# Six scatter views, adjacent x rows, later early weights and a new load order in a fused attention and expert kernel

## The chip, the cores and the metric

One core of one Trainium2 chip runs the kernel. The metric is device time in microseconds (us) of one execution; lower is better. The kernel before took 263.31, 264.16 and 266.78 us in three runs, median 264.16 us.

## The reference

Attention in chunks of 64 tokens feeds a mixture of eight experts with a capacity of 80 tokens each. All data is fp32: q, k and v are (8, 8, 576, 64), so x has 4608 rows (tokens) of 512.

```python
scores = scale * np.matmul(q_c, k_c.transpose(0, 1, 2, 4, 3))
scores = scores - np.max(scores, axis=-1, keepdims=True)
attn = np.exp(scores)
attn = attn / (np.sum(attn, axis=-1, keepdims=True) + 1e-09)
out = np.matmul(attn, v_c)
...
x = np.ascontiguousarray(attn_out.transpose(0, 2, 1, 3)).reshape(B * S, H * D)
...
logits = x @ w_gate
expert_idx = np.argmax(logits, axis=1)
...
gate_w = probs[np.arange(N), expert_idx]
out = np.zeros((N, D), dtype=np.float32)
for e in range(E):
    ...
    if len(tok_idx) > capacity:
        gw = gate_w[tok_idx]
        keep = np.argpartition(-gw, capacity)[:capacity]
        tok_idx = tok_idx[keep]
    h = np.maximum(x[tok_idx] @ w1[e], 0.0)
    out[tok_idx] = gate_w[tok_idx, None] * (h @ w2[e])
```

So at most 640 of the 4608 output rows are not zero.

## The kernel before

The program has three stages, written in a fixed order by hand (`manual_schedule`): each engine runs its own list, and SP's list is also the list of nearly all DMAs.

**Attention (lines 550 to 711).** 18 steps `j`, each of 256 tokens. A step loads q and k (`load_qk`, line 274: `qk` of 512 KB with c=0, and with c=1 `qz`, 256 KB twice, into one of two zero-padded tiles `kz`) and v (`load_v`, line 283: four loads of 130 KB into `vz`). PE makes scores (lines 297 and 303), DVE takes maxima and subtracts (310, 316), PE transposes (327, tile `pt`), ACT takes the exponential (335), PE multiplies with v into the PSUM tile `o` (345), DVE divides (361), and SP writes x to DRAM scratch `xs` (365, 512 KB). Step `i` of the loop at line 615 mixes scores of pair `i` with values of pair `i-2` and the transposes of pair `i-3` for the gate. Loads for pair `i+2` are issued in step `i`: first `qk`, then v of pair `i`, then `qz`. Each pair's buffers are two deep, so a load waits for PE to have read the pair two before. SP's list has eight DMAs per step, and each DMA of SP waits besides for the landing of the one eight before it. The gate's logits give each token an expert (`mine`) and a weight; GpSimd (POOL) writes per token a row of numbers `comp` (lines 449 to 459), five columns per expert: two parts of the row number, three parts of the gate weight.

**Choice (lines 704 to 856).** A threshold per expert, ranks, and matmuls that gather the chosen tokens' `comp` rows. From these come the row numbers `gi` and, for the first two of six row groups, the gather. Eight halves of the first two experts' weights (`early_weights`, 1 MB each) are issued at lines 671 (six) and 709 (two, both of w2 of expert 1).

**Experts (lines 859 to 900).** Six row groups `r` of 128 slots (96 per expert, so group 0 holds experts 0, 0, 0, 1, group 1 holds 1, 1, 2, 2, and so on). POOL gathers rows of `xs` (line 160), PE transposes, multiplies with w1 (`layer1`, line 185, two halves), transposes, multiplies with w2 (`layer2`, line 218), DVE scales with the gate (223) into one of four tiles `ys`, and POOL scatters the rows into `out` (line 227). Iteration `r` runs layer1 of group `r` and layer2 of group `r-1`. `ahead` (line 876) issues the remaining weights, 2 MB each, and the nine 1 MB zero writes to `out` (`clear`, line 535). The first of these weight loads is held behind the gather by a copy of one column of the gathered tile into the weight tile (line 873). All six scatters come after the zero writes in the program.

A branch behind the experts (line 903) handles inputs that overflow the fast path; here it is not taken.

## Time and profile before

| | |
|---|---|
| median of 3 runs | 264.16 us |
| profiled execution, its own time | 263.37 us |
| its span on the core | 261.5 us |
| PE busy | 221.5 us (85%) |
| DVE busy | 124.6 us (48%) |
| ACT busy | 72.1 us (28%) |
| POOL busy | 34.9 us (13%) |
| DMA moved | 85.02 MB, mean 325 GB/s |

The span is the time between the first and the last instruction of the program in the profile; the execution's own time is 1.87 us longer. Busy shares are means over three stages with different limits, so they are read by stage. "DMA share" is the mean busy share of the 16 DMA engines; PEclk is the granted TensorE clock as a share of full speed, 1.00 or 0.50. In a wait, `<-` names what ended it.

### The profile page before, as it was taken

Reading aid. Unit: us, or ns where it says so; the run is one execution under the profiler, and the core shown is the slowest. Engines: PE = TensorE matmul, PEld = TensorE weight load, DVE = VectorE, ACT = ScalarE, POOL = GpSimd, SP = SyncE. Lnnn points to the kernel's source line nnn. Section 1 sums busy time; section 2 is a strip of 40 time slices with the busy share of each in tenths; the row PEclk is TensorE's granted clock in tenths of the full one; section 3 lists DMA queues with packets and bytes.
Section 4 is the critical chain, followed back from the end, with each engine's and each line's share of the span. In section 5 each row is a group of like instructions: output and inputs, shape, how many; then the busy total and the mean of one; then the engine's idle time right before and its main releaser. Section 6 shows DMA issues by size and latency. Waiting matters only on the chain. (4 is left out here: it accounts for less than half of the span.)

```text
span 261.5 us, 7696 instructions
## 1 busy us (share of the span) xinstructions
PE 221.5 (85%) x3297; PEld 137.2 (52%) x3297; DVE 124.6 (48%) x343; ACT 72.1 (28%) x123; POOL 34.9 (13%) x101
## 2 busy tenths in 40 slices
PE   6379979989998999998996899999999999995000
PEld 5368858777786878787784244242332433321000
DVE  7438859786978688786779321021121112100100
ACT  1023335463737273856520012020010201000000
POOL 4110000101011011222423041000000000001331
PEclk9989999999999999999799799999999999999655
DMA  7997999999999999989998799999999999971110
GB/s 258 290 328 215 324 344 326 344 351 355 354 356 354 369 292 315 345 283 370 418 401 313 263 402 408 405 413 417 417 419 414 410 413 412 399 298 40 66 71 31
DMA packets 31496, 85.02 MB, mean 325 GB/s; under 512 B 3744, under 2 KB 3872, under 8 KB 31456
## 3 DMA queue, kind: packets, MB, share of 16 engines
q1 hardware_dynamic: 30192, 80.99, 84.1%
q0 software_dynamic: 960, 2.88, 3.1%
q8 instruction: 28, 0.46, 0.7%
q10 hardware_dynamic: 304, 0.59, 0.6%
q14 instruction: 12, 0.10, 0.1%
HBM read 64.27 MB, written 20.45 MB: 324 GB/s over the span
## 5 line engine op out<-in xcount | busy, mean ns | idle before, releaser
L185 PE MATMUL hc<-w,xtc 128*32 128x512 f32 x384 | 44.9, 611 | 0.2 <-ACT xtc L175 0.2
L218 PE MATMUL yc<-w,htc 128*32 128x512 f32 x384 | 42.3, 592 | 0.0
L345 PE MATMUL o<-vz,pT 128*64 128x130 f32 x576 | 35.9, 276 | 0.3 <-ACT pT L335 0.3
L310 DVE TENSOR_REDUCE mx<-s 128x8 f32<-128x512 f32 x36 | 23.2, 686 | 22.2 <-PE s L303 22.0
L345 PEld LDWEIGHTS o<-vz,pT 128*64 128x64 f32 x576 | 31.6, 135 | 1.5 <-ACT pT L335 0.5
L218 PEld LDWEIGHTS yc<-w,htc 128*32 128x32 f32 x384 | 12.4, 110 | 28.3 <-issue 28.3
L335 ACT ACTIVATE pT<-pt 128x1024 f32<-128x1024 f32 x18 | 18.4, 1023 | 31.2 <-PE pt L327 31.2
L185 PEld LDWEIGHTS hc<-w,xtc 128*32 128x32 f32 x384 | 12.8, 112 | 26.4 <-issue 25.9
L303 PE MATMUL s<-kz 128*64 128x128 f32 x288 | 20.9, 286 | 6.5 <-DMA kz<-in_qz 6.2
L374 ACT COPY xT<-px 128x1024 f32<-128x1024 f32 x18 | 18.2, 1012 | 25.5 <-PE px L327 25.5
L361 DVE TENSOR_TENSOR x<-o,rc 128x768 f32<-128x768 f32 (+1 forms) x36 | 23.2, 685 | 0.4
L223 DVE TENSOR_SCALAR ysc<-yc,gatec 128x512 f32<-128x512 f32 x6 | 4.5, 751 | 39.3 <-PE yc L218 24.7
L316 DVE TENSOR_TENSOR sm<-s,mx 128x512 f32<-128x512 f32 x36 | 22.9, 679 | 0.0
L190 ACT ACTIVATE hsc<-hc 128x512 f32<-128x512 f32 x6 | 3.6, 601 | 64.9 <-PE hc L185 64.9
L303 PEld LDWEIGHTS s<-kz 128*64 128x64 f32 x288 | 16.6, 141 | 8.4 <-issue 6.5
L227 POOL DMA_INDIRECT out<-ysc,si x6 | 6.0, 993 | 90.0 <-SPq L903 75.3
L297 PE MATMUL s<-qk 64*64 64x64 f32 x576 | 12.9, 229 | 3.8 <-issue 2.6
L297 PEld LDWEIGHTS s<-qk 64*64 64x64 f32 x576 | 10.5, 139 | 10.1 <-issue 7.6
L207 DVE COPY htc<-hpc 128x512 f32<-128x512 f32 x6 | 4.2, 692 | 21.3 <-PE hpc L203 21.3
L465 ACT ACTIVATE lv<-lev_t,own 128x256 bf16<-128x256 f32 x32 | 13.8, 498 | 0.9 <-DVE own L443 0.8
L192 DVE TENSOR_SCALAR hsc<-hc 128x512 f32<-128x512 f32 x6 | 4.2, 692 | 19.8 <-PE hc L185 19.8
L327 PE MATMUL px<-ct,x 64*128 64x64 f32 x288 | 12.9, 230 | 0.2 <-ACT pT L335 0.2
(157 smaller groups left out, 224.4 us busy)
## 6 DMA issues: line engine op xcount, KB each, us to landing
w<-in_w SPq DMA_DIRECT2D x12, 2048.0 KB, 21.2
vz<-in_vv SPq DMA_DIRECT2D x72, 130.0 KB, 4.9
qk<-in_qk SPq DMA_DIRECT2D x18, 512.0 KB, 5.6
xs<-x SPq DMA_DIRECT2D x18, 512.0 KB, 5.3
out<-zero SPq DMA_DIRECT2D x9, 1024.0 KB, 16.1
kz<-in_qz SPq DMA_DIRECT2D x34, 256.0 KB, 4.9
w<-in_w SPq DMA_DIRECT2D x8, 1024.0 KB, 14.2
kz<-in_qz ACTq DMA_DIRECT2D x2, 256.0 KB, 5.8
```

The costliest lines, as they stand in the source:

```text
L185: nc.tensor.matmul(h[o:o + 32, :], lhsT=xT[r][:, b, o:o + 32], rhs=getw(groups[r][g])[0][:, b, 512 * f:512 * f + 512], start=(b == 0), sto ...
L218: nc.tensor.matmul(y[o:o + 32, :], lhsT=hT[r][c // 4][:, c % 4, o:o + 32], rhs=getw(groups[r][g])[1][:, c, :], start=(c == 0), stop=(c == ...
L297: nc.tensor.matmul(s0[64 * u:64 * u + 64, h, pr], lhsT=q[64 * h:64 * h + 64, pr, u, :], rhs=k[64 * h:64 * h + 64, pr, u, :], start=True, s ...
L303: nc.tensor.matmul(s1[64 * u:64 * u + 64, :, pr], lhsT=z[:, pr, u, 1], rhs=z[:, pr, u, 0:3:2], start=True, stop=True)
L310: nc.vector.tensor_reduce(mx[:, :, 4 * c:4 * c + 4], PR[j]['s'][c], axis=AX.X, op=ALU.max)
L316: nc.vector.tensor_tensor(sm[:, 4 * c:4 * c + 4].rearrange("p a k h -> p h a k"), PR[j]['s'][c], PR[j]['mx'][:, :, 4 * c:4 * c + 4, None]. ...
L327: nc.tensor.transpose(pm[:, u, 64 * a:64 * a + 64], src(a)[rows], ident[rows, rows])
L335: nc.scalar.activation(pT, pm, AF.Exp, scale=0.125)
L345: nc.tensor.matmul(po[64 * u:64 * u + 64, a // 3, o:o + 130].rearrange("p (h x) -> p h x", h=2), lhsT=PR[j]['pT'][:, u, 64 * a:64 * a + 64 ...
L361: nc.vector.tensor_tensor(xf[:, lo:hi].rearrange("p (b m e) -> p b m e", b=b1 - b0, m=m), po[:, b0:b1, 0:m, 0:64], rc[:, b0:b1, 0:m, None] ...
L374: nc.scalar.copy(XT[T][:, j % 2].rearrange("p a u t -> p u a t"), pm.rearrange("p u (a t) -> p u a t", a=8))
L465: nc.scalar.activation(lv, lev_t[:, C_LEV:C_LEV + 2 * P], AF.Sign, bias=own[:, rt:rt + 1], scale=-1.0)
```

## The change

1. Each of the six scatters writes through its own view of `out`; the views are declared disjoint, so the program no longer makes one scatter wait for the one before.
2. `x` is written so that the two rows of one partition lie side by side in `xs` (4 KB in one piece in place of two pieces of 2 KB). The gather's row numbers change with it, so `comp` gets a sixth column per expert: `C_V`, the place within 256 rows.
3. The last two early weight halves (both of w2 of expert 1) are issued behind the first gather. The copy that holds back the weights now writes their tile.
4. Loads of the first pairs: all of pair 0 and 1 and v of pair 0 go out on SP in order of need, the constants move to step 2 (their use, `late_constants`, from step 2 to step 4), v of pair 1 is loaded in step 1, and in every step `qz` is issued right behind `qk` and ahead of v. Some memsets move from DVE to POOL. The scores of pair 1 go to tile `o` in place of `s`.

```diff
-    comp = cp.tile([P, RT, 5, NE], BF16, name="comp")
+    comp = cp.tile([P, RT, 6, NE], BF16, name="comp")
...
+        rows = dram_disjoint_views(out, NR) if extra else None
...
             nc.gpsimd.indirect_dma_start(
-                out=out, out_offset=bass.IndirectOffsetOnAxis(ap=si[:, r:r + 1], axis=0),
+                out=rows[r] if extra else out,
+                out_offset=bass.IndirectOffsetOnAxis(ap=si[:, r:r + 1], axis=0),
...
-            ps = ps1.tile([P, 2, 512], F32, name=f"s{j}", tag="s")
+            ps = S['o'][:, 0:2] if j == 1 else ps1.tile([P, 2, 512], F32, name=f"s{j}", tag="s")
...
-                xs[256 * j:256 * j + 256].rearrange("(c p) d -> p c d", c=2), x)
+                xs[256 * j:256 * j + 256].rearrange("(p c) d -> p (c d)", c=2), xf)
...
-                for j, c0 in ((0, C_A), (1, C_B)):
+                for j, c0 in enumerate((C_B, C_A, C_V)):
...
-        def early_weights(n):
+        def early_weights(n, after=None):
...
+            if after is not None:
+                nc.gpsimd.tensor_copy(w[:, 2 * j, 0:1], after)
...
-                    (nc.vector, nc.gpsimd)[b].memset(kz[b][:, o:o + 512], 0.0)
-            load_qk(0, 1, nc.scalar)
+                    (nc.vector if b == 0 and o == 0 else nc.gpsimd).memset(
+                        kz[b][:, o:o + 512], 0.0)
+            load_qk(0, 1)
             nc.scalar.dma_start(ident, cst[:, C_ID:C_ID + P])
...
+            for c in range(2):
+                load_qk(1, c)
...
-                    nc.vector.memset(vz[b, c], 0.0)
+                    (nc.gpsimd if b else nc.vector).memset(vz[b, c], 0.0)
+            for c in range(2):
+                load_v(0, c)
...
-                if i == 2:
+                if i == 4:
                     late_constants()
                 scores(i)
-                load_qk(i + 2, 0)
+                for c in range(2):
+                    load_qk(i + 2, c)
                 maxima(i)
...
-                if i >= 2:
+                if i >= 1:
                     for c in range(2):
                         load_v(i, c)
-                load_qk(i + 2, 1)
+                if i == 2:
+                    constants()
...
             divide(17)
-            for n in (6, 7):
-                early_weights(n)
             threshold(ph, misc[:, 1, 0:NE])
...
             def ahead(r, xg):
 
+                if r == 0:
+                    for n in (6, 7):
+                        early_weights(n, xg[0][:, 0:1] if n == 6 else None)
...
-                        part(e, l, xg[0][:, 0:1] if r + n == 0 else None)
+                        part(e, l)
```

**Where the instructions stand.** POOL at the end of the program, before. `xgc` is a gathered tile, `w` a weight tile, `ysc` a scaled result, DMASW and DMAHW are landings of POOL's and of SP's and ACT's DMAs.

```order
L160 DMA xgc_2791<-xs,gic_2656 128x512 [waits DMAHW2_49,DMAHW1_49,DMAHW5_49,DMAHW0_49,DVE_49]
L873 COPY w_2_2799<-xgc_2791 128x1 [waits DMAHW6_49,DMAHW7_49,DMAHW3_49,DMASW0_49]
...
L227 DMA out<-ysc_3014,si 4608x512 [waits DMAHW4_49,DMAHW3_49,DMAHW5_49,DMAHW1_49,DMAHW7_49,DMAHW0_49,DVE_49]
L227 DMA out<-ysc_3111,si 4608x512 [waits DMASW6_49,DVE_49]
L227 DMA out<-ysc_3214,si 4608x512 [waits DMASW7_49,DVE_49]
L227 DMA out<-ysc_3322,si 4608x512 [waits DMASW0_49,DVE_49]
L227 DMA out<-ysc_3425,si 4608x512 [waits DMASW1_49,DVE_49]
L227 DMA out<-ysc_3463,si 4608x512 [waits DMASW3_49,DMASW2_49,DVE_49]
```

The same place on POOL now.

```order
L163 DMA xgc_2797<-xs,gic_2662 128x512 [waits DMAHW2_49,DMAHW1_49,DMAHW5_49,DMAHW0_49,DVE_49]
L552 COPY w_1_2204<-xgc_2797 128x1 [waits DMASW0_49]
...
L230 DMA out<-ysc_3022,si 4608x512 [waits DMAHW4_49,DMAHW3_49,DMAHW5_49,DMAHW1_49,DMAHW7_49,DMAHW0_49,DVE_49]
L230 DMA out<-ysc_3119,si 4608x512 [waits DVE_49]
L230 DMA out<-ysc_3222,si 4608x512 [waits DVE_49]
L230 DMA out<-ysc_3330,si 4608x512 [waits DVE_49]
L230 DMA out<-ysc_3433,si 4608x512 [waits DVE_49]
L230 DMA out<-ysc_3471,si 4608x512 [waits DMASW3_49,DVE_49]
```

Scatters 1 to 4 lost their wait for a landing of POOL's DMAs; the last one keeps one. The first still waits for the zero writes.

SP's DMAs at the start, before (`kz` takes `qz`, `vz` takes v; ACT issued the two `qz` loads of pair 0):

```order
L278 DMA qk_103<-in_qk 128x1024
L278 DMA qk_166<-in_qk 128x1024
L281 DMA kz_108<-in_qz 64x1024 [waits Pool_49] x2
L286 DMA vz_119<-in_vv 64x520 [waits DVE_49]
...
L591 DMA ct<-in_cst 128x524 [waits DMAHW3_49]
L592 DMA lev_t<-in_cst 128x642 [waits DMAHW4_49]
...
L286 DMA vz_123<-in_vv 64x520 [waits DMAHW7_49,DVE_49]
...
L278 DMA qk_209<-in_qk 128x1024 [waits DMAHW3_49,PE_49]
```

SP's DMAs at the start now:

```order
L282 DMA qk_103<-in_qk 128x1024
L285 DMA kz_106<-in_qz 64x1024 [waits DVE_49]
L285 DMA kz_106<-in_qz 64x1024 [waits Pool_49]
L282 DMA qk_115<-in_qk 128x1024
L285 DMA kz_109<-in_qz 64x1024 [waits Pool_49] x2
L290 DMA vz_120<-in_vv 64x520 [waits DVE_49]
...
L282 DMA qk_201<-in_qk 128x1024 [waits DMAHW3_49,PE_49]
L285 DMA kz_106<-in_qz 64x1024 [waits DMAHW4_49,PE_49]
```

Pair 0 is complete ahead of pair 1, and pair 2 stands directly behind v of pair 0, with constants and v of pair 1 later.

SP around the gather, before (`w_0`, `w_1`, `w_2` are weights of experts 0, 1, 2):

```order
L547 DMA w_0_2194<-in_w 128x2x1024 [waits DMAHW7_49]
L547 DMA w_0_2194<-in_w 128x2x1024 [waits DMAHW0_49]
L365 DMA xs<-x_2290 128x2x512 [waits DMAHW1_49,DVE_49]
L365 DMA xs<-x_2402 128x2x512 [waits DMAHW2_49,DVE_49]
L547 DMA w_1_2198<-in_w 128x2x1024 [waits DMAHW3_49]
L547 DMA w_1_2198<-in_w 128x2x1024 [waits DMAHW4_49]
L874 DMA w_2_2799<-in_w 128x4x1024 [waits DMAHW5_49,PE_49,Pool_49]
```

SP around the gather now:

```order
L553 DMA w_0_2200<-in_w 128x2x1024 [waits DMAHW7_49]
L553 DMA w_0_2200<-in_w 128x2x1024 [waits DMAHW0_49]
L369 DMA xs<-x_2296 128x1024 [waits DMAHW1_49,DVE_49]
L369 DMA xs<-x_2409 128x1024 [waits DMAHW2_49,DVE_49]
L553 DMA w_1_2204<-in_w 128x2x1024 [waits DMAHW3_49,Pool_49]
L553 DMA w_1_2204<-in_w 128x2x1024 [waits DMAHW4_49]
L880 DMA w_2_2808<-in_w 128x4x1024 [waits DMAHW5_49,PE_49]
```

The wait for POOL's copy, and so for the gather, moved from the first weight of expert 2 to the last two halves of expert 1.

## Rows read from the trace of the kernel before

**Rows 1.** Timeline of POOL, gathers and scatters: start, duration, what, idle before.

```profile
139.76 1.27 POOL L160 DMA_INDIRECT xgc<-xs,gic  x1 [7.12 <-DVE bt L808]
144.30 0.19 POOL L873 COPY w<-xgc 128x1 f32<-128x1 f32 x1 [1.97 <-DMA xgc<-xs,gic]
...
153.21 1.00 POOL L160 DMA_INDIRECT xgc<-xs,gic  x1 [0.31 <-issue]
...
236.33 1.02 POOL L227 DMA_INDIRECT out<-ysc,si  x1 [75.33 <-SPq L903]
241.95 1.00 POOL L227 DMA_INDIRECT out<-ysc,si  x1 [4.60 <-DMA out<-ysc,si]
245.45 0.99 POOL L227 DMA_INDIRECT out<-ysc,si  x1 [2.50 <-DMA out<-ysc,si]
...
256.00 0.98 POOL L227 DMA_INDIRECT out<-ysc,si  x1 [2.49 <-issue]
```

**Rows 2.** Timeline of DVE, the scaling by the gate of groups 4 and 5.

```profile
241.26 0.75 DVE L223 TENSOR_SCALAR ysc<-yc,gatec 128x512 f32<-128x512 f32 x1 [11.82 <-PEq L903]
244.78 0.75 DVE L223 TENSOR_SCALAR ysc<-yc,gatec 128x512 f32<-128x512 f32 x1 [2.77 <-DMA out<-ysc,si]
```

**Rows 3.** Timeline of PE, expert stage.

```profile
144.38 0.63 PE L173 MATMUL xpc<-ct,xgc 128*128 128x128 f32 x4 [3.04 <-DMA xgc<-xs,gic]
...
145.26 5.16 PE L185 MATMUL hc<-w,xtc 128*32 128x512 f32 x32 [0.24 <-ACT xtc L175]
...
151.16 7.11 PE L185 MATMUL hc<-w,xtc 128*32 128x512 f32 x64
...
215.97 3.62 PE L185 MATMUL hc<-w,xtc 128*32 128x512 f32 x32
...
228.57 10.51 PE L218 MATMUL yc<-w,htc 128*32 128x512 f32 x96
```

**Rows 4.** Busy us by stretch: PE, PEld, DVE, ACT, POOL, then PEclk, DMA share, GB/s.

```profile
0.00:5.00 5.00, 2.88 (x14) 2.08 (x15) 3.54 (x7) 1.28 (x1) 2.87 (x15) 1.00 0.63 210
5.00:10.00 5.00, 3.14 (x61) 2.45 (x59) 2.02 (x4) 0.51 (x2) 0.00 (x0) 1.00 0.98 350
10.00:15.00 5.00, 2.89 (x48) 2.54 (x48) 2.01 (x4) 0.00 (x0) 2.44 (x7) 0.68 0.90 243
15.00:20.00 5.00, 3.52 (x76) 2.95 (x76) 2.48 (x4) 1.51 (x3) 0.00 (x0) 0.97 0.98 370
20.00:27.00 7.00, 6.79 (x148) 6.03 (x145) 6.61 (x12) 2.04 (x2) 0.00 (x0) 1.00 0.73 222
27.00:34.00 7.00, 6.72 (x150) 5.22 (x152) 5.87 (x12) 3.07 (x4) 0.00 (x0) 1.00 0.97 312
48.00:55.00 7.00, 6.34 (x137) 5.56 (x136) 5.41 (x15) 2.27 (x3) 0.90 (x5) 1.00 0.99 342
62.00:69.00 7.00, 6.90 (x152) 6.05 (x150) 6.44 (x18) 2.89 (x4) 0.44 (x2) 1.00 1.01 355
145.00:150.00 5.00, 4.76 (x33) 1.15 (x32) 1.26 (x7) 0.48 (x2) 0.00 (x0) 0.66 0.89 292
150.00:155.00 5.00, 5.00 (x76) 2.30 (x76) 0.77 (x6) 1.13 (x2) 2.52 (x3) 1.00 1.02 401
170.00:180.00 10.00, 10.00 (x96) 3.77 (x92) 2.14 (x3) 1.74 (x3) 0.00 (x0) 1.00 1.03 415
235.00:236.00 1.00, 1.00 (x16) 0.37 (x12) 0.00 (x0) 0.00 (x0) 0.00 (x0) 1.00 0.00 0
```

**Rows 5.** Waits from 20 to 118 us: us in total, times, longest.

```profile
PE s L303 <- DMA kz<-in_qz: 4.3, 6, 1.6
```

**Rows 6.** DMA summary of 229 to 233 us, where only zero writes move.

```profile
DMA packets 794, 1.60 MB, mean 399 GB/s; under 512 B 28, under 2 KB 28, under 8 KB 791
```

**Rows 7.** The `xs` tile: its writes (ns, first and last start), and DMA issue to landing.

```profile
L365 SPq DMA_DIRECT2D xs<-x x18: 383/537/2032, 25.5 to 123.3; - x18
...
DMA to landing us min/median/max: 3.6/5.4/16.7
```

More of the change, by code (lines that the diff above doesn't have):

```diff
@@ L6 @@
 from concourse._compat import with_exitstack
+from concourse.ap import dram_disjoint_views
 F32 = mybir.dt.float32
@@ L37 @@
 C_B = C_A + RT
-C_W8 = C_B + RT
+C_V = C_B + RT
+C_W8 = C_V + RT
 C_OOB = C_W8 + NE
@@ L114, in compact @@
     def compact(pool, pp, ptok, tag):
-        cand = pp.tile([P, 5, NE], F32, name=f"cand{tag}", tag="cand")
+        cand = pp.tile([P, 6, NE], F32, name=f"cand{tag}", tag="cand")
         for rt in range(RT):
@@ L123, in compact @@
                 start=(rt == 0), stop=(rt == RT - 1))
-        cb = pool.tile([P, 5, NE], BF16, name=f"cb{tag}", tag="cb")
+        cb = pool.tile([P, 6, NE], BF16, name=f"cb{tag}", tag="cb")
         nc.scalar.copy(cb, cand)
@@ L146, in targets @@
         gate, row, sv = (t[:, r0:r1] for t in tiles)
-        nc.vector.tensor_reduce(gate, pl[:, :, 2:5], axis=AX.X, op=ALU.add)
+        nc.vector.tensor_reduce(gate, pl[:, :, 3:6], axis=AX.X, op=ALU.add)
         nc.vector.tensor_reduce(row, pl[:, :, 0:2], axis=AX.X, op=ALU.add)
@@ L454, in parts @@
                         ct[:, c0 + rt:c0 + rt + n, None].to_broadcast(bc), op=ALU.mult)
[L455 to L458 removed]
+                p.tensor_copy(co[:, :, 3, :], kk)
+                p.tensor_tensor(r, kk, co[:, :, 3, :], op=ALU.subtract)
                 p.tensor_copy(co[:, :, 4, :], r)
+                p.tensor_tensor(r, r, co[:, :, 4, :], op=ALU.subtract)
+                p.tensor_copy(co[:, :, 5, :], r)
             return top, chosen, weight, key
@@ L551, in attention_moe @@
             load_qk(0, 0)
-            kz = {}
+            kz, vz = {}, {}
+            warm = gk.tile([P, 2 * P], BF16, name="warm", tag="lv", bufs=LV)
             for b in range(2):
@@ L555, in attention_moe @@
                 for o in (0, 1024):
-                    (nc.vector, nc.gpsimd)[b].memset(kz[b][:, o:o + 512], 0.0)
-            load_qk(0, 1, nc.scalar)
+                    (nc.vector if b == 0 and o == 0 else nc.gpsimd).memset(
+                        kz[b][:, o:o + 512], 0.0)
+            load_qk(0, 1)
             nc.scalar.dma_start(ident, cst[:, C_ID:C_ID + P])
-            io_h = gk.tile([P, P, HOT], BF16, name="io_h", tag="io_h", bufs=1)
-            lev_t = gk.tile([P, NLEV], F32, name="lev_t", tag="lev_t", bufs=1)
-            warm = gk.tile([P, 2 * P], BF16, name="warm", tag="lv", bufs=LV)
+            for c in range(2):
+                load_qk(1, c)
             nc.vector.memset(warm, 0.0)
-            nc.vector.memset(wgp[:, :, 8:32], 0.0)
-            vz = {}
             for b in range(2):
@@ L567, in attention_moe @@
                     vz[b, c] = wk.tile([P, 2, 520], F32, name=f"vz{b}{c}", tag=f"vz{b}{c}", bufs=1)
-                    nc.vector.memset(vz[b, c], 0.0)
+                    (nc.gpsimd if b else nc.vector).memset(vz[b, c], 0.0)
+            for c in range(2):
+                load_v(0, c)
+            io_h = gk.tile([P, P, HOT], BF16, name="io_h", tag="io_h", bufs=1)
+            lev_t = gk.tile([P, NLEV], F32, name="lev_t", tag="lev_t", bufs=1)
+            nc.vector.memset(wgp[:, :, 8:32], 0.0)
             pw = ps2.tile([P, 256], F32, name="pw", tag="g")
@@ L586, in attention_moe, with constants @@
                 nc.gpsimd.memset(rsts[r0][:, :, 0:1], 0.0)
-            for c in range(2):
-                load_qk(1, c)
-            for c in range(2):
-                load_v(0, c)
-            nc.sync.dma_start(ct[:, C_ID + P:], cst[:, C_ID + P:NCONST])
-            nc.sync.dma_start(lev_t, cst[:, NCONST:])
-            nc.sync.dma_start(wgp[:, :, 0:8], wg.rearrange("(b p) e -> p b e", p=P))
-            nc.sync.dma_start(capi, cap[0:1, :].broadcast_to([P, 2]))
-            for c in range(2):
-                load_v(1, c)
+            def constants():
+                nc.sync.dma_start(ct[:, C_ID + P:], cst[:, C_ID + P:NCONST])
+                nc.sync.dma_start(lev_t, cst[:, NCONST:])
+                nc.sync.dma_start(wgp[:, :, 0:8], wg.rearrange("(b p) e -> p b e", p=P))
+                nc.sync.dma_start(capi, cap[0:1, :].broadcast_to([P, 2]))
             nc.scalar.copy(id_b, ident)
@@ L747, in listed @@
                 nc.vector.tensor_reduce(
-                    kc, cand[:, 2:5, :].rearrange("p c e -> p e c"), axis=AX.X, op=ALU.add)
-                cb = mp.tile([P, 5, NE], BF16, name=f"cb{nm}", tag=f"cb{nm}")
+                    kc, cand[:, 3:6, :].rearrange("p c e -> p e c"), axis=AX.X, op=ALU.add)
+                cb = mp.tile([P, 6, NE], BF16, name=f"cb{nm}", tag=f"cb{nm}")
                 nc.scalar.copy(cb, cand)
@@ L793, in spread @@
                                         lists[n][0][:, e:e + 1].to_broadcast([P, P]), ident)
-            cands.append(ps2.tile([P, 5, NE], F32, name="candb", tag="g"))
+            cands.append(ps2.tile([P, 6, NE], F32, name="candb", tag="g"))
             gather_up(cands[1], [*range(LATE, RT)], 0, 4)
@@ L891, in remaining @@
             def remaining(pp):
-                pl, gi = place(mp, pp.tile([P, NR - 2, 5], F32, name="pl2", tag="y", bufs=1),
+                pl, gi = place(mp, pp.tile([P, NR - 2, 6], F32, name="pl2", tag="y", bufs=1),
                                pairs, "c", 2, NR)
@@ L970, in attention_moe @@
                         cand, cb = compact(xp, lp, ptok, "g")
-                        pl = place(xp, lp.tile([P, NR, 5], F32, name="gpl", tag="pl"),
+                        pl = place(xp, lp.tile([P, NR, 6], F32, name="gpl", tag="pl"),
                                    lambda e, j: [
@@ L1009, in _constants @@
     row = 128 * rt + p
-    c[:, C_A:C_A + RT] = row // 64 * 64
-    c[:, C_B:C_B + RT] = row % 64
+    c[:, C_A:C_A + RT] = row // 256 * 256
+    c[:, C_B:C_B + RT] = row % 256
+    c[:, C_V:C_V + RT] = 2 * p + rt % 2
     c[:, C_W8:C_W8 + NE] = NE - np.arange(NE)
```

10 lines of the change are left out of this document (3 added, 7 removed).

## The prediction

> **What bounds the kernel now.** I read the DMA share by stretch first, since 85 MB in 261.5 us suggest a kernel near its memory rate, then the timelines of POOL and PE in the last third.
>
> In [rows 4] the DMA engines are busy all the time at 342 to 355 GB/s in the middle of attention and at 415 GB/s in the expert stage, but not at the start: 243 GB/s from 10 to 15 us, 222 (share 0.73) from 20 to 27. Attention is bound by its loads, with PE close behind (6.34 and 6.90 of 7 us). PE waits 4.3 us in all for `qz` loads [rows 5].
>
> The expert stage has two streams that end together: PE, dense at 10.00 of 10 us [rows 4], whose last matmul ends at 228.57 + 10.51 = 239.1 [rows 3], and the DMA stream of twelve 2 MB weight loads with nine 1 MB zero writes behind and between, empty from 235 us on [rows 4].
>
> Then nothing computes for 22.4 us. [Rows 1] show why: six scatters, the first at 236.33 when the zeros have landed, the second 4.60 us after the first ends, the others about 2.50 us after the one before. With 1 us each that is 3.5 us a scatter. The last starts at 256.00 and ends at 256.98; 4.5 us later the span ends. Scaling by the gate hangs in the same chain: groups 4 and 5 wait for a `ys` tile, so for the landing of scatters 0 and 1 (DVE at 241.26, 3.9 us after scatter 0 ended, and at 244.78, 1.8 us after scatter 1 ended [rows 1, 2]).
>
> **Scatters.** The order shows that scatters 1 to 4 lose their wait for a landing, and the last one's remaining wait is for a DMA of POOL eight back in its round of landings, a gather long done. What is late next is POOL itself and the tiles. Two POOL DMAs with nothing between start 0.31 + 1.00 = 1.31 us apart (153.21 [rows 1]). Let the first scatter start at time t. Scatters 1 to 3 start at t + 1.3, 2.6 and 3.9. Scatter 0 ends at t + 1.0 and its tile is free at t + 4.9 (by 3.9) or t + 2.8 (by 1.8); I take the 3.9, measured on that very scatter. Scaling takes 0.75, so scatter 4 starts at t + 5.7. Scatter 1 ends at t + 2.3 and frees its tile at t + 4.1 to 6.2; with 6.2 and 0.75 scatter 5 starts at t + 7.0. By the faster landing POOL's spacing decides: t + 6.6. From scatter 5 on it is 0.98 + 4.5 as before. So first scatter to end: 25.2 us before (261.5 − 236.33), 12.5 now: **−12.7**. Bounds: −13.1 by the faster landing; if scatters side by side in the queue each land as late as the first one did, the last ends 2 us later: −10.7.
>
> **Weights behind the gather.** Two halves, 2 × 1.05 = 2.1 MB, no longer fill the queue while the choice is computed; they join the stream that ends with the zeros. At 415 GB/s they are 5.1 us. In return the gather runs alone. Before it took 144.30 − 141.03 = 3.27 us from POOL's end to the copy that waits for it, beside those two loads; a scatter alone takes 2.5 from end to the next start [rows 1]. I take the difference, −0.8 (bounds 0 and −1.6, half of the 3.27, since a scatter's row is a write). It does not start earlier: it waits for the last x write, issued at 123.3 [rows 7], which has six weight halves ahead of it in both kernels (16.7 us for the slowest [rows 7]); the two moved halves were behind it. Sum for the end of the zeros, so for t: **+4.3** (bounds +3.5 and +5.1).
>
> The Trainium skill, page "DMA: Bandwidth & Descriptors", section "Specifications", puts the HBM limit per core at about 358 GB/s. By that rule the 2.1 MB would cost 5.9 us and the sum would be 0.8 us worse. This case's trace disagrees: 415 GB/s over ten us [rows 4].
>
> PE pays too. Group 1's first half needs w1 of expert 2, which now stands behind the 2.1 MB. Before, PE came to it half way through the row at 151.16, at 154.7 [rows 3]. The stream moved 5 × 0.292 = 1.46 MB by 150 and 2.0 MB more by 155 [rows 4]; 4.2 MB are reached at 156.8, minus 0.8 is 156.0, plus up to 2.5 until the landing is known. PE comes there later by 1.3 to 3.8 us. After the idle 3.04 us at 144.38 [rows 3] PE's clock was granted at half (0.66 on average from 145 to 150 [rows 4]), and the half group there took 5.16 us in place of 3.62; a stall may cost that 1.5 again. I take +3.3 of 1.3 to 5.3. Later rounds keep their order and move as one: a round of PE is (215.97 − 154.7) / 4 = 15.3 us [rows 3], and 4/3 experts are 5.6 MB or 13.5 us of stream.
>
> This stall hides. PE would end at 239.1 + 3.3 = 242.4, with the front's gain off that. Scatter 5 needs PE's end plus 0.9 and starts at t + 7.0, with t = 236.33 + 4.3 = 240.6, so at 247.6. The cover is 4 us; beyond a stall of 7.6 us every further one counts in full.
>
> **The front.** By 34 us the stream had moved 5 × (0.210 + 0.350 + 0.243 + 0.370) + 7 × (0.222 + 0.312) = 9.6 MB [rows 4]. At 348 GB/s, between the two steady rows, that is 27.6 us, and the idle 0.37 of the first 5 us is start-up (1.9): 29.5, so 4.5 us are holes. The new order can fill them: SP's list is no longer held at v of pair 2, behind which `qz` of later pairs stood, pair 1's scores wait for no tile, and the constants (0.6 MB) are out of the first pairs' way until their use in step 4. Eight landings stay in flight, so it is the waits on PE, two pairs back, that could open a hole again. I take all 4.5 of it (bounds 0, where PE or SP make the same hole later, and 4.5 + 4.3 = 8.8, were all waits for `qz` gone besides).
>
> **Adjacent x rows** halve the packets of a quarter of attention's traffic. Zeros go out in 2 KB packets (1.60 MB in 794) at 399 GB/s [rows 6], the weights at 415: 4% of a quarter of 6 us is 0.06 us a step, about 1 us in 18. I take −0.5 (0 to −1.1), as PE leaves little room. The sixth column is one POOL instruction more per gate on an engine busy 0.44 to 0.90 of 7 us [rows 4], hidden by DVE's chain; in the last gate it delays the row numbers by some 0.2 us, which the wait for the x write covers, and costs 0.2 if not. The moved memsets run before the first loads land.
>
> **Sum**, against the profiled execution: −4.5 − 0.5 + 4.3 − 12.7 = −13.4. The span becomes 248.1 and the execution 263.37 − 13.4 = 250.0 us. The profiled one lies 0.8 under the median of 264.16, so a median may come out at 250.8; I name 250.0, since the terms are no finer.
>
> **Rivals.**
>
> *The front gives nothing* (−0.5 in place of −5): SP still holds eight loads and waits for PE two pairs back, and PE is busy 6.9 of 7 us in the middle, so a lead may be eaten by the time attention ends. Against it: the holes are in the stream that bounds. Time 254.5. Chance 0.20.
>
> *More at the front* (−8.8, x rows at −1.1): all `qz` waits go as well, since `qz` now stands ahead of v. Time 263.37 − 8.8 − 1.1 + 4.3 − 12.7 = 245.1. Chance 0.11.
>
> *The scatters do not overlap*: the order frees them, but one queue and its landing times keep them 3.5 us apart, and only the front and the stream count: 263.37 − 5 + 4.3 = 262.7. For it: the first took 4.60 us to its successor. Against it: gathers 1.31 us apart on the same queue. Chance 0.05.
>
> *Slower: weights late in every round.* The stream behind the gather has 1.8 us of room per 15.3 us round, and it holds the zeros too. If layer2 of group 0 waits for the moved halves and layer1 in each of the five later rounds for its w1, 5.3 us each (stall and half clock), PE ends at 239.1 − 5 + 32 = 266 and the execution at 266 + 0.9 + 0.98 + 4.5 + 1.9 = 274. It decides once the stalls pass 7.6 us in sum, and makes the kernel slower than before from 21 us, 3.5 us each. Against it: PE waited for no weight in the expert stage (10.00 of 10 [rows 4]). Chance 0.04.
>
> **How the numbers follow.** The forecast has 0.60 and its own range is 247 to 253.5. The range of 244.5 to 256 takes in the first two rivals as well and leaves out about 0.15. A measurement of this kernel tells about 2% from no change, so faster means under 258.9 and slower over 269.4: faster is 0.60 + 0.20 + 0.11 = 0.91, within 2% 0.05, slower 0.04.
>
> **What would show it.** POOL's scatters 0 to 3 should stand 1.3 us apart and the last start some 7 us after the first. PE should wait 2 to 5 us for a weight in its second round and never again for more than 2. DMA should move about 345 GB/s between 10 and 34 us. The gap in the DMA stream around the gather should be wider than before. The prediction is wrong if scatters stay 3.5 us apart, if the first gather does not start near 135 us (139.76 less 5), or if PE and not the scatters ends last.

## The result and the profile after

The changed kernel took 252.83 us in the median of four runs (251.57 to 254.69) against 264.60 us for the kernel before on the same chip; the ratio is 0.9553, 95% interval 0.9464 to 0.9642. In a second comparison it took 251.12 us against 264.35 (0.9463, 0.9392 to 0.9533). The forecast was 250.0 us, with a range of 244.5 to 256.0. Ratios, here and below, leave out disturbed runs that the medians hold; that matters for one kernel (qz early only). The profiled execution took 251.57 us with a span of 249.7 us; before it was 263.37 and 261.5.

The timeline of POOL of the changed kernel (start, duration, what, idle before), the answer to [rows 1]:

```profile
133.51 1.27 POOL L163 DMA_INDIRECT xgc<-xs,gic  x1 [6.73 <-DVE bt L814]
...
137.86 0.18 POOL L552 COPY w<-xgc 128x1 f32<-128x1 f32 x1 [1.77 <-DMA xgc<-xs,gic]
...
235.84 1.02 POOL L230 DMA_INDIRECT out<-ysc,si  x1 [73.08 <-SPq L912]
237.16 1.00 POOL L230 DMA_INDIRECT out<-ysc,si  x1 [0.30 <-issue]
...
239.76 0.98 POOL L230 DMA_INDIRECT out<-ysc,si  x1 [0.30 <-DVE ysc L226]
241.05 0.98 POOL L230 DMA_INDIRECT out<-ysc,si  x1 [0.30 <-issue]
244.01 0.98 POOL L230 DMA_INDIRECT out<-ysc,si  x1 [1.98 <-DVE ysc L226]
```

Five scatters stand 1.30 us apart, where [rows 1] had 5.62 and 3.50; the sixth comes 8.2 us after the first, and 4.7 us go by from its end to the end of the span (249.7 − 244.99). In the profile of the second comparison the sixth comes 6.5 us after the first, and 6.2 us go by behind it (251.9 − 245.75):

```profile
238.28 1.02 POOL L230 DMA_INDIRECT out<-ysc,si  x1 [73.69 <-SPq L912]
...
244.77 0.98 POOL L230 DMA_INDIRECT out<-ysc,si  x1 [0.30 <-issue]
```

In the first profile the first gather starts 6.25 us earlier, but the first scatter only 0.5 us earlier: what the front gave was spent between the two.

DVE's timeline, the answer to [rows 2], and the chain of work that ended last say what the sixth scatter of the first profile waited for:

```profile
238.64 0.75 DVE L226 TENSOR_SCALAR ysc<-yc,gatec 128x512 f32<-128x512 f32 x1 [7.44 <-DMA out<-ysc,si]
242.98 0.75 DVE L226 TENSOR_SCALAR ysc<-yc,gatec 128x512 f32<-128x512 f32 x1 [3.59 <-remote]
```

```profile
239.93 0.02 DVEq L226
239.95 3.01 another core or an unknown queue
242.98 0.76 DVE ysc L226
```

The scaling of group 5 at 242.98 needs two things: the landing of scatter 1, whose tile it takes, and PE's last matmul. The wait of DVE's queue (DVEq) for the landing is over at 239.95, 1.8 us after scatter 1 has ended on POOL (238.16). What it then waits 3.0 us for is PE. PE's last matmul ends at 240.84, but the signal that PE raises for it stands in the trace at 242.96, 2.1 us later; in the other profiles below it comes 0.04 us after that end, and 0.33 us in the one without the branch. "remote" and "unknown queue" mean that the profile found no releaser close enough to name. Why the signal was late this once is open.

PE's timeline, the answer to [rows 3]:

```profile
153.82 6.20 PE L188 MATMUL hc<-w,xtc 128*32 128x512 f32 x28 [4.58 <-DMA w<-in_w]
...
230.33 10.51 PE L221 MATMUL yc<-w,htc 128*32 128x512 f32 x96
```

PE stops for 4.58 us in the first half of group 1, where w1 of expert 2 is due, and the 28 matmuls after it take 6.20 us; at the 7.11 us for 64 of [rows 3] they would take 3.1. It ends at 240.84, 1.8 us later than before although it began 6 us earlier.

The stretches of the changed kernel (columns as in [rows 4]):

```profile
10.00:15.00 5.00, 3.52 (x77) 2.79 (x73) 2.93 (x5) 1.02 (x1) 0.00 (x0) 1.00 0.98 366
20.00:27.00 7.00, 7.00 (x154) 6.21 (x150) 6.36 (x12) 3.55 (x5) 1.48 (x3) 1.00 0.90 289
130.00:135.00 5.00, 5.00 (x55) 3.96 (x53) 4.42 (x25) 0.00 (x0) 1.27 (x1) 1.00 0.23 93
135.00:140.00 5.00, 2.31 (x17) 1.01 (x18) 4.76 (x31) 0.65 (x2) 1.19 (x2) 0.86 0.48 125
150.00:155.00 5.00, 1.18 (x8) 0.40 (x12) 0.00 (x0) 0.00 (x0) 0.00 (x0) 0.72 1.01 382
155.00:160.00 5.00, 5.00 (x25) 0.99 (x17) 0.00 (x0) 0.00 (x0) 0.00 (x0) 0.59 1.03 417
170.00:180.00 10.00, 10.00 (x96) 3.79 (x92) 1.44 (x2) 1.74 (x3) 0.00 (x0) 1.00 1.03 410
```

The holes at 10 to 15 and 20 to 27 us are smaller (366 and 289 GB/s for 243 and 222); over all of 10 to 34 us DMA moved 341 GB/s for 284. In their place stands a wide one around the gather, 93 and 125 GB/s from 130 to 140. The kernel before had a narrower one there:

```profile
140.00:145.00 5.00, 1.96 (x17) 1.37 (x14) 4.89 (x32) 0.17 (x1) 2.22 (x3) 1.00 0.62 208
```

After the stall PE's granted clock averages 0.72 and then 0.59, between the two levels of 1.2 and 2.4 GHz, and full again later.

### The profile page after: what moved, and what is told of

The parts are those of the page before. It is cut to its first block, busy times and chain, and to the rows that moved or that the text cites. A ratio compares the mean times of both kernels' runs of the same rounds, so it can differ in the third digit from the quotient of the medians.

```text
span 249.7 us, 7719 instructions
## 1 busy us (share of the span) xinstructions
PE 223.7 (90%) x3297; PEld 136.2 (55%) x3297; DVE 122.0 (49%) x340; ACT 71.9 (29%) x123; POOL 38.9 (16%) x113
## 5 line engine op out<-in xcount | busy, mean ns | idle before, releaser
L188 PE MATMUL hc<-w,xtc 128*32 128x512 f32 x384 | 48.6, 641 | 4.8 <-DMA w<-in_w 4.6
L314 DVE TENSOR_REDUCE mx<-s 128x8 f32<-128x512 f32 x34 | 21.9, 684 | 19.9 <-PE s L307 19.9
L320 DVE TENSOR_TENSOR sm<-s,mx 128x512 f32<-128x512 f32 x34 | 21.6, 677 | 0.0
L307 PE MATMUL s<-kz 128*64 128x128 f32 x272 | 19.1, 279 | 2.2 <-DMA kz<-in_qz 1.8
L307 PEld LDWEIGHTS s<-kz 128*64 128x64 f32 x272 | 14.9, 136 | 4.0 <-issue 2.4
L301 PEld LDWEIGHTS s<-qk 64*64 64x64 f32 x544 | 10.0, 134 | 9.3 <-issue 4.6
L301 PE MATMUL s<-qk 64*64 64x64 f32 x544 | 12.4, 225 | 2.9 <-DMA qk<-in_qk 1.7
L456 POOL TENSOR_TENSOR comp<-mine,ct 128x32 bf16<-128x32 bf16 x27 | 5.7, 238 | 48.3 <-DVE mine L443 48.3
## 6 DMA issues: line engine op xcount, KB each, us to landing
kz<-in_qz SPq DMA_DIRECT2D x36, 256.0 KB, 5.6
out<-zero SPq DMA_DIRECT2D x9, 1024.0 KB, 16.2
```

Source lines behind the costliest of these rows:

```text
L188: nc.tensor.matmul(h[o:o + 32, :], lhsT=xT[r][:, b, o:o + 32], rhs=getw(groups[r][g])[0][:, b, 512 * f:512 * f + 512], start=(b == 0), sto ...
L301: nc.tensor.matmul(s0[64 * u:64 * u + 64, h, pr], lhsT=q[64 * h:64 * h + 64, pr, u, :], rhs=k[64 * h:64 * h + 64, pr, u, :], start=True, s ...
L307: nc.tensor.matmul(s1[64 * u:64 * u + 64, :, pr], lhsT=z[:, pr, u, 1], rhs=z[:, pr, u, 0:3:2], start=True, stop=True)
L314: nc.vector.tensor_reduce(mx[:, :, 4 * c:4 * c + 4], PR[j]['s'][c], axis=AX.X, op=ALU.max)
L320: nc.vector.tensor_tensor(sm[:, 4 * c:4 * c + 4].rearrange("p a k h -> p h a k"), PR[j]['s'][c], PR[j]['mx'][:, :, 4 * c:4 * c + 4, None]. ...
```

## The experiments

Every trace is cut in three legs at the same two marks: G, the start of the first gather, and t, the start of the first scatter. G is what the front does, t − G the stream of weights and zeros, "end − t" the scatters with what follows up to the end of the span. A fourth column is PE's last matmul against G. All from the timelines of POOL and PE and the span of one profiled execution each; the medians and ratios are from all runs.

| kernel | median us | before beside it | ratio, 95% interval | G | t − G | end − t | PE's end − G |
|---|---|---|---|---|---|---|---|
| before | 264.16 | | | 139.76 | 96.57 | 25.17 | 99.3 |
| changed | 252.83 | 264.60 | 0.9553, 0.9464 to 0.9642 | 133.51 | 102.33 | 13.86 | 107.3 |
| changed again | 251.12 | 264.35 | 0.9463, 0.9392 to 0.9533 | 136.62 | 101.66 | 13.62 | 106.1 |
| views only | 251.31 | 264.50 | 0.9514, 0.9448 to 0.9579 | 140.57 | 96.50 | 11.73 | 98.6 |
| front only | 259.77 | 264.50 | 0.9817, 0.9744 to 0.9890 | 135.46 | 97.10 | 25.44 | 99.7 |
| all but the views | 263.06 | 264.50 | 0.9944, 0.9895 to 0.9993 | 135.38 | 101.53 | 23.99 | 106.9 |
| all but part 3 | 246.82 | 264.50 | 0.9325, 0.9246 to 0.9405 | 135.03 | 97.63 | 11.74 | 99.9 |
| all but part 3, again | 248.28 | 264.65 | 0.9380, 0.9318 to 0.9442 | 136.81 | 97.26 | 12.33 | 100.4 |
| all but adjacent x | 253.60 | 264.35 | 0.9559, 0.9488 to 0.9629 | 137.13 | 101.36 | 13.01 | 106.4 |
| all, qz late | 256.26 | 264.35 | 0.9635, 0.9552 to 0.9719 | 139.75 | 101.46 | 13.19 | 105.5 |
| qz early only | 262.86 | 264.65 | 0.9844, 0.9772 to 0.9915 | 137.68 | 96.94 | 25.68 | 99.7 |
| all, w1 first | 251.44 | 264.35 | 0.9508, 0.9437 to 0.9580 | 136.10 | 101.75 | 11.75 | 103.2 |
| all, no branch | 251.12 | 265.54 | 0.9523, 0.9431 to 0.9616 | 135.45 | 101.96 | 10.49 | 105.2 |
| part 3 undone, zeros early | 248.95 | 264.65 | 0.9416, 0.9349 to 0.9483 | 134.82 | 94.13 | 17.05 | 103.4 |

The middle leg repeats far better than the whole: t − G lies within 1 us over all seven profiles with part 3. G is the noisy one, 133.51 and 136.62 for the same changed kernel. One execution's total is therefore good to some 2 us, and the legs decide.

### The views alone, and all but the views

Views only: of the changes, the kernel before gets this.

```diff
+        rows = dram_disjoint_views(out, NR) if extra else None
...
-                out=out, out_offset=bass.IndirectOffsetOnAxis(ap=si[:, r:r + 1], axis=0),
+                out=rows[r] if extra else out, out_offset=bass.IndirectOffsetOnAxis(ap=si[:, r:r + 1], axis=0),
```

> The kernel before with part 1 alone. Theory (the tail alone is worth more than the rest of the change together): the first scatter stays at 236.3 us, the last starts 8 us after it, 251.5 to 253.5 us in all, as fast as the whole change. Rival (the parts add up, so one alone gives its own term): 255 us or more.

All but the views: the changed kernel with these lines undone.

> The changed kernel with part 1 alone undone: all scatters write through the whole output again. Theory (the waits for landings were the tail): scatters 3.5 us apart from 235.8 us on, the last near 254 to 255 us, 261 to 263 us in all. Rival (the queue moves one scatter's rows in about 1.5 us whatever the waits, and the end hangs on PE): 254 to 256 us.

The views alone save 13.2 us by medians (264.50 − 251.31), and the last leg falls from 25.17 to 11.73. The last scatter starts 6.5 us after the first, where 8 were expected:

```profile
237.07 1.02 POOL L229 DMA_INDIRECT out<-ysc,si  x1 [76.00 <-SPq L905]
...
243.55 0.98 POOL L229 DMA_INDIRECT out<-ysc,si  x1 [0.30 <-issue]
```

Without them the changed kernel keeps 1.4 us (264.50 − 263.06). Its POOL timeline shows the old spacing:

```profile
236.91 1.02 POOL L230 DMA_INDIRECT out<-ysc,si  x1 [72.73 <-SPq L912]
240.41 1.00 POOL L230 DMA_INDIRECT out<-ysc,si  x1 [2.48 <-DMA out<-ysc,si]
...
255.30 0.98 POOL L230 DMA_INDIRECT out<-ysc,si  x1 [2.50 <-issue]
```

So the wait for the landing of the scatter before is the whole of this term, and one queue with its landings does not keep the scatters apart.

### The front alone, and which part of it

Front only: part 4 in the kernel before (the sixth column stays, x is not adjacent, the weights stay ahead of the gather).

> The kernel before with the new load order and memsets alone (parts 1, 2 and 3 undone in the changed kernel; the sixth column stays). Theory (holes in the stream at the start are filled and the lead lasts): the first gather starts 5 to 6.5 us before 139.8, the scatters stay 3.5 us apart, 257 to 259.5 us in all. Rival (the lead comes from x rows written in 4 KB pieces): the gather starts at 138 us or later and the time is 262 us or more.

It saves 4.7 us (264.50 − 259.77), nearly all of it in G (4.3 us in the profiles, for the 5 to 6.5 expected). Then part 4 was cut in two. "qz late" is the changed kernel with

```diff
-                for c in range(2):
-                    load_qk(i + 2, c)
+                load_qk(i + 2, 0)
...
+                load_qk(i + 2, 1)
```

> The changed kernel with qz issued behind v again in every step of attention's loop; the new order of the first two pairs and the later constants stay. Theory (the front's gain is the hole from 10 to 34 us being closed by the new order at the start): 0 to 1.5 us slower, first gather at 133.5 to 135, PE's waits for qz from 20 to 118 us back to 3 to 5 us in all without a loss of the same size. Rival (the gain is qz standing ahead of v in the loop): 3 us or more slower, first gather at 136.5 or later, DMA under 320 GB/s between 20 and 34 us.

and "qz early only" is the opposite move in the kernel before, with its old start.

> The kernel before with a single move: qz is issued right behind qk in attention's loop, ahead of v; start order, constants, memsets and everything else as before. Theory (new, since the kernel with qz late lost the whole lead: the hole at 20 to 27 us comes from qz standing behind v in the loop): 3 to 6 us faster than before (258.5 to 261.5), first gather at 134 to 137.5 in place of 139.8, DMA from 20 to 27 us at 260 GB/s or more in place of 222. Rival (both the start order and the loop order are needed, one alone closes nothing): within 1.5 us of before, first gather at 138.5 or later.

Stretches from 10 to 27 us, first qz late, then qz early only:

```profile
10.00:15.00 5.00, 2.15 (x45) 1.63 (x49) 2.82 (x5) 1.02 (x1) 0.00 (x0) 1.00 0.96 340
15.00:20.00 5.00, 4.45 (x75) 4.31 (x64) 2.07 (x4) 0.00 (x0) 0.00 (x0) 0.66 0.79 257
20.00:27.00 7.00, 6.91 (x175) 6.04 (x172) 6.27 (x13) 3.06 (x3) 0.00 (x0) 1.00 0.77 215
```

```profile
10.00:15.00 5.00, 2.89 (x64) 2.41 (x64) 2.94 (x6) 0.00 (x0) 2.41 (x7) 0.85 0.87 235
20.00:27.00 7.00, 7.00 (x127) 6.52 (x124) 4.59 (x9) 1.03 (x1) 0.00 (x0) 0.76 0.85 272
```

With qz late the hole at 10 to 15 is closed (340 GB/s for 243), but the one at 20 to 27 is open (215), a new one stands at 15 to 20 (257 for 370), and G is 139.75, as before the change: the theory put to the run, that the start order carries the gain, fell. With qz early and the old start it is the other way round (235 and 272). G gains 2.1 us, and the time 1.8 us by medians or 4.1 us by the ratio (2.2 to 6.0), where 3 to 6 were expected.

Over 10 to 34 us DMA moved 284 GB/s before, 274 with qz late, 296 with qz early only, and 303 to 342 in the ten profiles with all of part 4. So `qz` ahead of v is needed: without it the lead is lost. That the start order adds to it is what G and the DMA rate say; the ratios of the front alone (0.9817) and of qz early only (0.9844) do not tell the two apart.

### Part 3 undone

The two halves are issued ahead of the choice again; the rest of the change stays.

```diff
             divide(17)
+            for n in (6, 7):
+                early_weights(n)
...
-                if r == 0:
-                    for n in (6, 7):
-                        early_weights(n, xg[0][:, 0:1] if n == 6 else None)
...
-                        part(e, l)
+                        part(e, l, xg[0][:, 0:1] if r + n == 0 else None)
```

> The changed kernel with part 3 alone undone: the two halves of expert 1's w2 are issued again behind x's last write, ahead of the gather. Theory (part 3 costs twice: 2.1 MB more in the stream that ends with the zeros, and a stall of PE in its second round): the first gather stays near 133.5 us, PE does not wait for weights in round two and ends near 233 in place of 240.8 us, the first scatter starts near 231 in place of 235.8 us, the last about 8 us later, and the execution takes 246 to 248 us. Rival (part 3 pays, because the gather or the last x write comes earlier when the two halves are out of the way): the first gather starts or lands 1 to 2 us later than 133.5 and 137.8 us and the time is 252 us or more.

> The kernel without part 3 (two weight halves ahead of the gather again) once more, beside the two others of this job. Every theory: 246 to 248 us, some 5 us below the changed kernel (251.1 and 252.8 in its two jobs).

246.82 and 248.28 us: faster than both kernels, and by 4 to 6 us in the first of the comparisons (252.83 and 251.12 for the changed kernel), by 3 to 5 in the second. The kernels with and without part 3 were not compared on one chip, and some of the intervals of the ratios overlap; the middle leg decides. t − G falls from 102.33 and 101.66 to 97.63 and 97.26, and end − t from 13.86 and 13.62 to 11.74 and 12.33. PE waits for no weight in the expert stage. The rival, a gather that comes earlier with the halves behind it, does not show: G is 135.03 and 136.81 here, 133.51 to 137.13 with part 3 and all of part 4. The first of the two timelines of POOL:

```profile
135.03 1.27 POOL L163 DMA_INDIRECT xgc<-xs,gic  x1 [6.85 <-DVE bt L816]
...
139.97 0.19 POOL L881 COPY w<-xgc 128x1 f32<-128x1 f32 x1 [2.36 <-DMA xgc<-xs,gic]
...
232.66 1.02 POOL L230 DMA_INDIRECT out<-ysc,si  x1 [75.85 <-SPq L911]
...
239.15 0.99 POOL L230 DMA_INDIRECT out<-ysc,si  x1 [0.30 <-issue]
```

The last scatter starts 6.5 us after the first, five steps of 1.30, where about 8 were expected.

### The same bytes in another order

w1 of expert 2 goes first behind the gather, then the two halves.

```diff
-                if r == 0:
-                    for n in (6, 7):
-                        early_weights(n, xg[0][:, 0:1] if n == 6 else None)
...
-                        part(e, l)
+                        part(e, l, xg[0][:, 0:1] if r + n == 0 else None)
+                        if r + n == 0:
+                            for k in (6, 7):
+                                early_weights(k)
```

> The changed kernel with the two halves held behind the gather exchanged in place with the load behind them: w1 of expert 2 (2 MB) goes first, then the two halves of w2 of expert 1. The same bytes move behind the gather; only what PE waits for first differs. Theory (PE's stall in its second round is what makes part 3 dear in PE's time, but most of it is hidden, because the zero writes end at 235.8 in any case): the wait of layer1 for in_w at 154 goes or falls under 1.5 us, PE ends 3 us or more earlier than 240.8, the first scatter stays at 235 to 236.5, and the execution gains only 1 to 3 us (249 to 251), since what is left is the last scatter set by POOL's spacing from the first one. Rival (the stall counts in full): the execution gains 5 us or more, 247 or less. Rival (the stall only moves, since layer2 of group 0 needs the moved halves as early): no gain.

PE's timeline of this kernel:

```profile
145.31 7.11 PE L188 MATMUL hc<-w,xtc 128*32 128x512 f32 x64
...
167.64 5.08 PE L188 MATMUL hc<-w,xtc 128*32 128x512 f32 x30 [2.48 <-DMA w<-in_w]
```

The stall at 154 is gone, 2.5 us of it come back a round later, and PE ends 3 us sooner after G (103.2 for 106.1). t − G is unchanged: the zeros end the stream whatever PE does. The time is that of the changed kernel beside it (251.44 and 251.12 us), so the gain of 1 to 3 us that was expected did not show in the medians; in the legs end − t fell by 1.9 us, and G happened to be close (136.10 and 136.62).

### Adjacent x rows undone

```diff
-                xs[256 * j:256 * j + 256].rearrange("(p c) d -> p (c d)", c=2), xf)
+                xs[256 * j:256 * j + 256].rearrange("(c p) d -> p c d", c=2), x)
...
-    c[:, C_V:C_V + RT] = 2 * p + rt % 2
+    c[:, C_V:C_V + RT] = row % 256
```

> The changed kernel with part 2 undone: x goes to memory in two pieces of 2 KB per partition, the sixth column stays and gives the gather the plain row number. Theory (parts 1 and 4 alone add up to what the kernel without part 3 gained, so adjacent rows are worth next to nothing): 0 to +1.1 us against the changed kernel of this job, first gather 0 to 1.1 us later than 133.5. Rival (adjacent rows carry part of the front's gain, which came out larger than forecast): 2 us or more slower, first gather behind 135.5.

> The changed kernel once more, unaltered, beside the three others of this job, so that they are compared with it on one chip. Every theory: about 252 us (250.5 to 254).

253.60 us against 251.12 for the unaltered kernel beside it, with overlapping intervals; G is 137.13 against 136.62. The medians lean to the rival, the traces (0.5 us) to the theory. This stays open; against the rival speaks that the views and the front alone give 13.2 + 4.7 = 17.9 us, and all but part 3, which has adjacent rows besides, 17.7 and 16.4.

### Zeros ahead of the gather

On the kernel without part 3, three of the nine zero writes go out behind the early weights, ahead of the choice, to fill the gap in the stream.

```diff
             for n in (6, 7):
                 early_weights(n)
+            for z in range(3):
+                clear(z)
...
-                                clear(z)
+                                if z >= 3:
+                                    clear(z)
```

> The kernel without part 3 and with three of the nine zero writes (3 MB) issued ahead of the gather, behind the early weights, so that the DMA stream does not run dry while the choice is computed. Theory (while the choice is computed the DMA engines stand still for some 3 to 5 us whatever the kernel, and bytes put there come off the end of the stream): the first scatter starts 93 to 96 us after the first gather in place of 97.6, PE's end stays at 99 to 101 us after it and then sets the last scatter, and the execution is 1 to 3 us under the kernel of this job without them (244 to 246). Rival (the gather shares the engines with the zeros, so every us gained behind is lost ahead of it): the copy that waits for the gather comes 1.5 us or more later after the gather's start than without the zeros, PE ends as much later, and the execution gains nothing or loses up to 3 us.

```profile
134.82 1.27 POOL L163 DMA_INDIRECT xgc<-xs,gic  x1 [7.18 <-DVE bt L818]
...
142.06 0.18 POOL L883 COPY w<-xgc 128x1 f32<-128x1 f32 x1 [4.67 <-DMA xgc<-xs,gic]
...
239.33 0.98 POOL L230 DMA_INDIRECT out<-ysc,si  x1 [4.21 <-DVE ysc L226]
```

The rival held. t − G falls by 3 us as the theory said, but the copy that waits for the gather comes 6.0 us after the gather's end (142.06 − 136.09) in place of 3.5 to 3.7, PE ends 3 us later after G (103.4 for 100.4), and the last scatter now waits for PE. 248.95 us against 248.28 without the zeros: nothing gained.

### The branch left out

The changed kernel ends with the last scatter; the path for inputs that overflow, not taken here, is left out.

```diff
-    with tc.If(nc.values_load(flag_i[0:1, 0:1], min_val=0, max_val=1) > 0):
...
```

> The changed kernel without the branch behind the experts: the path for inputs that overflow, which is not taken here, is left out, so that little code follows the last scatter. Theory (near PE's end two 16 KB packets of instructions are loaded through one of the 16 DMA engines and hold up that engine's five packets of the scatters behind them, so two landings are known late, the tile of group 5 comes free 2.1 us after PE's last matmul, and the last scatter starts 8.2 us after the first): without the branch at most one such packet moves in the last 12 us, group 5 is scaled within 0.5 us of PE's end, the last scatter starts 6.4 to 7.0 us after the first, and the execution is 1 to 3 us under the changed kernel (248.5 to 251). Rival (landings of scatters side by side take 3 us or more by themselves, whatever else moves): group 5 is still scaled 1.5 us or more after PE's end and the last scatter starts 7.5 us or more after the first, at the same time as the changed kernel within 1 us.

What led to it: a list of DMA queues names "instruction" packets of 16 KB in the last microseconds. The branch stands behind the last scatter in the program. The list for the kernel before, from 237.5 to 241 us (GB/s in 40 equal slices, then packets, MB and share of the 16 engines by queue; q0 carries POOL's indirect DMAs):

```profile
GB/s 0 0 0 0 468 188 469 234 515 187 375 187 0 0 0 0 0 0 0 0 0 0 0 0 47 0 0 0 0 47 0 0 47 0 47 0 0 0 0 0
...
q0 software_dynamic: 80, 0.23, 18.0%
q8 instruction: 1, 0.02, 3.2%
```

The 80 packets are scatter 0. Nearly all move within 0.8 us, up to 238.6; the last five follow one by one a microsecond later. The same list for 237.7 to 238.2 us holds the instruction packet, and that for 239.6 to 240.8 the five stragglers:

```profile
q8 instruction: 1, 0.02, 22.2%
```

```profile
q0 software_dynamic: 5, 0.02, 5.5%
```

By its share the packet takes 1.8 us (22.2% of 16 engines over 0.5 us). So it comes with the scatter's packets, and a sixteenth of them (5 of 80, the share of one DMA engine) waits behind it. That is why the tile came free only after 3.9 us [rows 1, 2]. The changed kernel from 237 to 249.7, then the same without the branch from 237 to 248:

```profile
GB/s 0 297 335 90 0 219 349 155 52 181 297 103 0 194 374 181 13 181 323 245 0 0 13 13 26 0 52 361 207 26 0 0 26 0 0 0 0 0 0 0
...
q8 instruction: 2, 0.03, 1.0%
q14 instruction: 3, 0.02, 0.7%
```

```profile
GB/s 0 0 0 0 0 0 0 343 313 179 0 0 402 298 134 0 149 357 209 0 0 224 417 194 0 0 402 298 134 0 149 328 239 0 0 0 0 0 0 0
...
q0 software_dynamic: 480, 1.31, 31.0%
```

Without the branch no such packet moves, and six equal bursts stand with no stragglers. Its timelines of POOL and DVE:

```profile
237.41 1.02 POOL L230 DMA_INDIRECT out<-ysc,si  x1 [74.86 <-DMA out<-zero]
...
243.90 0.98 POOL L230 DMA_INDIRECT out<-ysc,si  x1 [0.30 <-issue]
```

```profile
241.56 0.75 DVE L226 TENSOR_SCALAR ysc<-yc,gatec 128x512 f32<-128x512 f32 x1 [0.58 <-DMA out<-ysc,si]
```

Group 5 is scaled 1.8 us after scatter 1's end (239.74) and 0.9 us after PE's (230.13 + 10.51 = 240.64); half a microsecond was expected, and the remaining wait is that landing. The last scatter starts 6.5 us after the first, but that does not speak for the theory: it does so with the branch too, in the second profile of the changed kernel. The theory's reading of the first profile, a tile of group 5 held by a late landing, does not hold either, since that landing was known at 239.95 and PE's signal was what came late.

end − t is 10.49 in place of 13.86 and 13.62. From the last landing to the end of the span 2.6 us go by in all thirteen profiles with the branch and 1.3 us here, so 1.3 us are the end of the program itself. In the first profile of the changed kernel most of the rest is the late start of the sixth scatter (8.2 for 6.5 us). In the second it is the late landing of the sixth, 3.6 us after its end for 1.7 here: a 16 KB packet moves from 245.8 to 247.3 there, and the last five packets of scatters 4 and 5 each follow behind it, up to 248.9. That a packet of instructions holds up landings is therefore seen in the traces; what leaving it out saves besides the 1.3 us depends on which scatter it meets. The three profiles with the branch that end soonest after t have 11.73 to 11.75, just 1.3 us more than here.

The median, 251.12 us, is inside the spread of the changed kernel's two, so the gain of 1 to 3 us that was expected is shown in the leg and not in the total.

## Why the prediction was right, and where it was wrong

The forecast's terms of the front, the weights and the scatters came out close, the stall of PE did not, but it stayed hidden; 250.0 us are 1.6 under the profiled execution and 1 to 3 under the medians. Part of this is luck: in that execution the front gave 1.3 us more than the 5.0 taken, and t − G took 1.5 us more than the 4.3 (102.33 − 96.57 = 5.8).

- **The front** (−5.0 with adjacent rows): over the ten profiles with all of part 4 the mean G is 135.6, over the two with none of it (before, views only) 140.2: −4.5. In the one execution compared above it was −6.25. The mechanism named first, `qz` held behind v, is shown to be needed; what the start order adds to it is not settled. From 10 to 34 us DMA moved 303 to 342 GB/s, for the 345 forecast. The rival by which the front gives nothing is out, and so is the larger lead, 9.9 us.
- **Weights behind the gather** (+4.3): t − G is 97.0 in the mean of six profiles without part 3 (the one with early zeros left out) and 101.7 in seven with it, +4.7. Both halves of the term hold. The gather ends 2.5 to 3.1 us before the copy when alone and 3.3 to 3.7 us beside the two loads, in the means of the same profiles 0.9 sooner (0.8 taken). From the copy to t it is 5.6 us longer (97.8 for 92.2), where 5.1 were taken. The limit of about 358 GB/s for a core's HBM traffic that the Trainium skill gives, page "DMA: Bandwidth & Descriptors", section "Specifications", makes 2.1 MB an estimated 5.9 us. The trace stands between that and the 5.1: 2.1 MB in 5.6 us are 375 GB/s, while 410 GB/s are held from 170 to 180 us, so what the half microsecond more was is open.
- **Scatters** (−12.7): −11.3, since the last leg is 13.86 (13.62 in the second profile) and not 12.5. The spacing of 1.3 us and the fourth scatter came as written (t + 3.9), the fifth sooner (t + 5.2 for 5.7). The step that was mis-sized is the tile free 3.9 us after its scatter ends. The 3.9 us were not a property of scatters: a landing takes about 1.8 us, as the second line of [rows 2] has it, and up to 4.3 us where an instruction packet holds up one engine. Scatter 1's was known 1.8 us after its end, so the sixth scatter had only POOL's spacing to wait for, t + 6.6, which the prediction gave as its bound. That is what the second profile shows (t + 6.5), and the five others with views, branch and neither `qz` late nor early zeros. In the first it came at t + 8.2, for PE's late signal, which the sum does not have. The other half, 4.5 us from the sixth's end to the end of the span, was 4.7 in the first profile and 6.2 in the second, where its landing was late. So the 12.5 is near both for reasons that it did not name, and that is luck.
- **PE's stall** (+3.3, bounds 1.3 to 5.3): PE's end − G rose by 6.6 us (99.6 in the mean of six, 106.2 of six). This is the term that was mis-sized, twofold. The weight was expected 16.2 to 18.7 us after G and came after 20.3 (153.82 − 133.51; 19.1 to 20.3 in the six profiles), because the sum took all that DMA moves as bytes that PE needs. The list of queues of the changed kernel from 137 to 154 us says what else moved:

```profile
q1 hardware_dynamic: 1246, 4.91, 76.0%
q0 software_dynamic: 300, 1.01, 16.4%
...
w<-in_w SPq DMA_DIRECT2D x6, 2048.0 KB, 27.3
```

  Beside the 4.2 MB that PE needed went 0.7 MB of later weights, since six loads of 2 MB were in the queue at once, and 1.0 MB of gathers. And the clock cost not 1.5 but 3.1 us (6.20 for 28 matmuls; 5.0 to 6.2 in the six profiles, so 1.9 to 3.1).
- **"This stall hides"**: nearly. PE ends 5.0 us after t in the changed kernel and 1.5 us after it with w1 first, and t − G is the same. But end − t is 13.0 to 13.9 in the four profiles with views and branch where PE ends 4.0 to 5.0 us after t, and 11.7 to 12.3 in the four where it ends 1.5 to 3.2 us after t. In every profile with the branch a 16 KB packet of instructions starts 0.5 to 1.2 us before PE's end and another 2.2 to 3.6 us after it, so a late PE pushes them into the last scatters. The landings behind them are late in the traces; the longer leg of the first profile is PE's late signal instead. That PE's end moves the leg through these packets is argued, not shown: no run moves the packets alone, and without the branch PE ends sooner after t as well (3.2 us).
- **Weights late in every round**, the slower rival: the profile has a single wait for a weight, 4.6 us (6.5 in the second). It did not come.

So part 3 is the one part shown to lose, and the forecast had its sign right (+4.3 of stream); that the kernel is better without it, by 3 to 6 us, follows from the same sum.
